# Linear attention with a SoLU feed-forward on one core: weights converted in 1024-column pieces, and a new written-out order

## The chip, the cores and the metric

The kernel runs on one core of a Trainium2 chip. The metric is the device time in microseconds (us); the lower the better. PE is the matrix engine (TensorE), DVE the vector engine, ACT the scalar engine (ScalarE), POOL is GpSimd, and SP issues the DMAs. Each engine works through its own instructions strictly in order.

## The reference

```python
# q, k, v: (8 batches, 8 heads, 576, 64) float32; the weights are float64
q_s = softmax(q, axis=-1)                    # exp(q - max), divided by the sum + 1e-9
k_s = softmax(k, axis=2)                     # over the 576 positions
kv  = einsum('bhsd,bhse->bhde', k_s, v)
x   = einsum('bhsd,bhde->bhse', q_s, kv)     # then to (8 * 576, 512)
h   = x @ w_in                               # (4608, 1024)
solu = h * softmax(h, axis=-1)
ln  = (solu - mean) / sqrt(var + 1e-6) * g_ln
out = ln @ w_out                             # (4608, 512)
```

## The kernel before

The work is cut into 36 row tiles of 128 rows: four for each of the 8 batches, and one for each pair of batches, made of the 64 rows that each has left over. There is one generator for each piece of work, and one step of a generator issues one or a few instructions. The string `ORDER` (1,509 items) says, by hand, which generator makes its next step; a suffix `.v` or `.p` moves that step's elementwise instruction to DVE or POOL. So the order on every engine, and often the engine, is written out in `ORDER`.

The names in it, and in the rows below:

- `LQ`, `LK`, `LV`, `V`, `LG`: loads of q, k, v and of the gain. `Q0a`, `Q1c`, `R1`: softmax of q (tiles `qm`, `qr`, maxima `qnmx`, sums `qsum`), split into a high and a low float16 half (`qhl`) and transposed by DMA into `qT`.
- `K0`: k's softmax of batch 0 (`km`, and `kr` for the 64 left-over rows; `khalf` and `ktop` are its maxima, `turned`, `col`, `wide`, `kb` carry them across partitions), the products `kv` with v, and its two float16 halves in a block diagonal (`bd`).
- `w0`, `w1`, ...: a piece of w_in. The host's float64 arrives as pairs of 32-bit words (tile `w_in`), and `float_of` puts a float32 together from them in `iw`: one instruction on ACT, a clamp on POOL or DVE, a shift and two merges on DVE. `W` scales w_in by a power of two and splits it into a high and a low float16 half (`wi`); it needs the largest value of the whole matrix (`m_in`), so all of w_in has to be converted first. `y0`, `y1`, ... and `Z` are the same for w_out (`w_out`, `gw`, `wo`).
- `x3`, `h3`, `o3`: for row tile 3 the product with `kv` (`xT`), the hidden layer with SoLU and the centred values (`h`, its maximum `top`, `nm`, `e`, `u`, transposed by DMA into `uT`), and the projection (`o`, `os`). Each of the products of `h` and `o` is three float16 products. `h` has two buffers in PSUM, `o` one.
- `P`: four products on zeros, to keep PE busy (`warm_up`).

For each tile of `h`, four single-column steps (`am`, `pi`, `p`, `ph`) run mostly on POOL, between DVE's `nm` and DVE's product `e`.

`BUFS` holds the number of buffers of `uT`, `xT` and of the words of a weight. The buffers of `uT` (4 KB in each partition) also hold w_in's words and the float32 weights.

## Time and profile before

| | |
|---|---|
| median of 3 runs | 533.48 us (533.06 to 534.55) |
| profiled execution, its own time | 535.23 us |
| its span, first to last instruction | 533.5 us |
| busy: PE, DVE, ACT, POOL | 475.2, 427.7, 270.4, 192.7 us |

Busy time is the time in which an engine executes an instruction; what matters is whether the engine that others wait for is busy at that place. In the page's picture of the span in 40 slices (busy tenths; PEclk is the clock that was granted to PE), the first quarter looks different from the rest:

```profile
PE   4652579889999999999999999999989999999886
DVE  4999999998899899899999999388978764635711
PEclk9576699998999999999999999999999999999999
```

### The profile page before, as it was taken

The numbers are of one execution on the slowest core, as the hardware profiler recorded it, in microseconds if no ns is written. First come the engines' busy times: TensorE is split into PE (matmuls) and PEld (weight loads), VectorE is DVE, ScalarE is ACT, GpSimd is POOL, SyncE is SP. The second block draws the span as 40 slices with busy tenths as digits, with TensorE's granted clock in tenths as the row PEclk, the third lists the DMA queues.
The fourth block names the chain that finished last, engine by engine and source line by source line (L and its number), as shares of the span: only waits on it lengthen the run. The fifth ranks groups of instructions, "written<-read, shape, count | busy, mean of one in ns | idle before, by whom it ended". The sixth has DMA issues, their size and how long they took to land.

```text
span 533.5 us, 8255 instructions
## 1 busy us (share of the span) xinstructions
PE 475.2 (89%) x3048; PEld 243.5 (46%) x3048; DVE 427.7 (80%) x724; ACT 270.4 (51%) x405; POOL 192.7 (36%) x309
## 2 busy tenths in 40 slices
PE   4652579889999999999999999999989999999886
PEld 1330245444454445455545455454445554544334
DVE  4999999998899899899999999388978764635711
ACT  2375556766474573456545656166645552424600
POOL 4522156543433550446334434054641321211210
PEclk9576699998999999999999999999999999999999
DMA  8963952992359957945965897179247443232251
GB/s 229 336 174 117 256 122 53 267 175 39 80 131 245 215 100 164 247 104 119 236 159 90 208 187 169 39 132 224 59 104 187 78 98 80 39 80 61 54 123 41
DMA packets 159240, 74.99 MB, mean 141 GB/s; under 512 B 127840, under 2 KB 152672, under 8 KB 159200
## 3 DMA queue, kind: packets, MB, share of 16 engines
q1 hardware_dynamic: 159200, 74.47, 62.1%
q8 instruction: 24, 0.39, 0.3%
q14 instruction: 16, 0.13, 0.1%
HBM read 36.70 MB, written 9.44 MB: 86 GB/s over the span
## 4 chain that ended last, share of the span: by engine, by line
PE 41%; DVE 38%; issue 8%; POOL 5%; ACT 4%; DMA 2%; SPq 0%; DVEq 0%; POOLq 0%; ACTq 0%
PE o L590 21%; PE h L519 17%; DVE e L548 4%; DVE top L526 4%; DVE km L356 3%; DMA qm<-in_q_dram 2%; DVE qsum L419 2%; DVE u L555 2%; POOL p L542 2%; DVE bd L395 2%; DVE qhl L430 1%; DVE qnmx L412 1%; DVE iw L237 1%; PE x L471 1%; DVE qden L421 1%
## 5 line engine op out<-in xcount | busy, mean ns | idle before, releaser
L519 PE MATMUL h<-wi,xT 128*128 128x512 f16 x864 | 196.4, 381 | 4.5 <-DVE e L548 4.0
L590 PE MATMUL o<-wo,uT 128*128 128x512 f16 (+1 forms) x888 | 194.2, 373 | 6.4 <-DVE os L598 4.2
L590 PEld LDWEIGHTS <-uT 128*128 128x128 f16 x888 | 85.9, 98 | 102.5 <-issue 7.6
L519 PEld LDWEIGHTS <-xT 128*128 128x128 f16 x864 | 83.7, 98 | 102.3 <-issue 3.2
L553 ACT ACTIVATE u<-e,nmu 128x1024 f16<-128x1024 f32 x36 | 41.3, 1148 | 33.8 <-DVE nmu L550 32.4
L526 DVE TENSOR_REDUCE top<-h 128x1 f32<-128x1024 f32 x36 | 43.8, 1216 | 17.3 <-PE h L519 17.2
L532 ACT ACTIVATE e<-h,nm,hs 128x1024 f32<-128x1024 f32 x32 | 38.5, 1203 | 33.3 <-DVE nm L528 32.0
L562 ACT ACTIVATE e<-e,nmu 128x1024 f32<-128x1024 f32 x36 | 41.2, 1146 | 25.7 <-DVE u L555 25.2
L555 DVE SCALAR_TENSOR_TENSOR u<-e,nmu,u 128x1024 f16<-128x1024 f32 x36 | 47.3, 1317 | 6.7 <-ACT u L553 6.7
L548 DVE SCALAR_TENSOR_TENSOR e<-h,ph,e 128x1024 f32<-128x1024 f32 x36 | 46.0, 1279 | 4.9 <-POOL ph L545 2.5
L575 POOL TENSOR_TENSOR r<-var,mhalf 128x1 f32<-128x1 f32 x36 | 24.4, 677 | 69.9 <-DVE var L572 63.6
L598 DVE TENSOR_SCALAR os<-o,rr 128x512 f32<-128x512 f32 (+1 forms) x21 | 15.2, 724 | 31.6 <-PE o L590 25.6
L503 ACT ACTIVATE xT<-x 128x512 f16<-128x512 f32 x36 | 21.2, 591 | 33.3 <-PE x L471 23.9
L542 POOL TENSOR_TENSOR p<-pi,mone 128x1 f32<-128x1 f32 x36 | 24.2, 673 | 34.1 <-DVE pi L539 32.5
L536 POOL TENSOR_SCALAR am<-nm 128x1 f32<-128x1 f32 x23 | 9.7, 422 | 67.7 <-DVE nm L528 67.6
L373 PE MATMUL kv<-vm,km 128*64 128x65 f32 x512 | 23.0, 234 | 7.5 <-ACT km L358 5.4
L471 PE MATMUL x<-qT,bd 128*128 128x128 f16 x128 | 23.8, 225 | 5.1 <-DVE bd L395 5.1
L416 ACT ACTIVATE qm<-qm 128x1024 f32<-128x1024 f32 (+1 forms) x17 | 17.1, 1007 | 19.4 <-DVE qm L414 12.7
L425 POOL TENSOR_TENSOR qm<-qm,qrec 128x1024 f32<-128x1024 f32 (+1 forms) x10 | 18.3, 1833 | 20.6 <-DVE qrec L423 12.9
L645 PE MATMUL warm_up<-bd 128*128 128x512 f16 x60 | 23.5, 535 | 2.3 <-POOL bd L127 1.7
L373 PEld LDWEIGHTS kv<-vm,km 128*64 128x64 f32 x512 | 18.5, 143 | 14.2 <-ACT km L358 5.9
L414 POOL TENSOR_TENSOR qm<-qm,qnmx 128x1024 f32<-128x1024 f32 (+1 forms) x8 | 15.3, 1907 | 25.9 <-DVE qnmx L412 21.4
(140 smaller groups left out, 698.8 us busy)
## 6 DMA issues: line engine op xcount, KB each, us to landing
...
w_in<-in_moe_w_in_dram SPq DMA_DIRECT2D x8, 512.0 KB, 9.2
w_out<-in_moe_w_out_dram SPq DMA_DIRECT2D x8, 512.0 KB, 5.5
out_dram<-os SPq DMA_DIRECT2D x10, 128.0 KB, 2.4
qm<-in_q_dram SPq DMA_DIRECT2D x2, 512.0 KB, 4.8
```

The source lines that it names most:

```text
L373: nc.tensor.matmul(o, km[:, h + i, c], vm[:, h + i, c], start=(c == 0), stop=False)
L471: nc.tensor.matmul(acc, al, bh, start=False, stop=True)
L519: nc.tensor.matmul(h[:, ns], xT[:, t, kc], wi[:, s, kc, ns], start=(kc == 0 and t == 0 and s == 0), stop=(kc == NP - 1 and t == 1),)
L526: nc.vector.tensor_reduce(top, h, axis=AX.X, op=ALU.max, negate=True)
L532: nc.scalar.activation(e, h, AF.Exp, bias=nm, scale=hs, accum_out=z)
L542: nc.gpsimd.tensor_tensor(p, pi, mone, op=ALU.pow)
L548: nc.vector.scalar_tensor_tensor(e, h, ph, e, op0=ALU.mult, op1=ALU.mult, accum_out=s1)
L553: nc.scalar.activation(u[:, 0], e, AF.Identity, bias=nmu)
L555: nc.vector.scalar_tensor_tensor(u[:, 1], e, nmu, u[:, 0], op0=ALU.add, op1=ALU.subtract)
L562: nc.scalar.activation(e, e, AF.Square, bias=nmu, accum_out=s2)
L575: nc.gpsimd.tensor_tensor(r, var, mhalf, op=ALU.pow)
L590: nc.tensor.matmul(o, uT[:, j, f], wo[:, s, f, cols], start=(f == 0 and j == 0 and s == 0), stop=(f == NF - 1 and j == 1))
```

## The change

Weights are loaded and converted in pieces of 1024 columns, so there are four pieces of w_in and four of w_out where there were eight of each. A piece is loaded by two DMAs of 512 KB, one step each, into one of two buffers of its own. In `float_of` the absolute value and the clamp go; ScalarE multiplies by 2^-112, which moves the exponent, and keeps the sign. The largest value of w_out is taken per piece and multiplied by the larger of the two gains. The products that spread k's maxima and the other single values over the partitions are issued as transposes. In `hidden`, the products with w_in's low half come last. The warm-up products write to the buffers of `h`. The order string is new (1,619 items).

```diff
-BUFS = 14, 4, 3
+BUFS = 12, 4, 2
 ORDER = (
-    "LG LQ0*2 w1 LK0*3 LV0 w0 w2 V00 V01 Q0b LV1 Q0b.v w4 Q0c Q0b w5 w7 Q0b Q0c w6 Q0a y0 y1 K0 Q0c y2 "
...
+    "LQ0*2 w0 Q0a Q0a.v LK0 w0 Q0b Q0a*2 Q0c w0 K0 w1 Q0a LK0 w0 Q0a K0 Q0b*2 w0*2 w1 V02 w2 Q0c Q0b "
...
     def largest(x, wide, name):
-        nc.tensor.matmul(wide, x.broadcast_to([P, P]), ident, start=True, stop=True)
+        nc.tensor.transpose(wide, x.broadcast_to([P, P]), ident)
...
-    def load_words(src, rows, cols, name, tag, bufs):
-        w = sb.tile([P, WN, 2], I32, name=f"w_{name}", tag=tag, bufs=bufs)
-        nc.sync.dma_start(out=w, in_=src[rows, 2 * cols.start : 2 * cols.stop].rearrange("p (n two) -> p n two", two=2))
-        return w
+    def load_words(src, n, name):
+        w = sb.tile([P, DF, 2], I32, name=f"w_{name}", tag="wd", bufs=WB)
+        for i, x in enumerate(src):
+            c = slice(i * n, (i + 1) * n)
+            nc.sync.dma_start(out=w[:, c], in_=x.rearrange("p (n two) -> p n two", two=2))
+            yield w
...
     def float_of(words, x):
-        nc.scalar.activation(x, high.bitcast(F32), AF.Abs)
-        yield
-        on(nc.gpsimd).tensor_scalar(x, x, 3.0e38, 1.125 * 2.0**-15, op0=ALU.min, op1=ALU.max)
-        yield
-        nc.vector.tensor_scalar(xi, xi, 3, 0x3FFFFFFF, op0=ALU.logical_shift_left, op1=ALU.bitwise_and)
+        nc.scalar.activation(x, high.bitcast(F32), AF.Copy, scale=2.0**-112)
+        yield
+        nc.vector.tensor_scalar(xi, xi, 3, 0x7FFFFFFF, op0=ALU.logical_shift_left, op1=ALU.bitwise_and)
         yield
         nc.vector.scalar_tensor_tensor(xi, low, 29, xi, op0=ALU.logical_shift_right, op1=ALU.bitwise_or)
         yield
-        nc.vector.scalar_tensor_tensor(xi, high, -0x40000000, xi, op0=ALU.bitwise_and, op1=ALU.bitwise_or)
+        nc.vector.scalar_tensor_tensor(xi, high, -0x80000000, xi, op0=ALU.bitwise_and, op1=ALU.bitwise_or)
...
-    def weight_in(i):
+    def weight_in(kc):
+        rows = slice(kc * P, (kc + 1) * P)
+        for words in load_words([w_in[rows, i * DF : (i + 1) * DF] for i in range(2)], DF // 2, f"in{kc}"):
+            yield
+        x = iw[kc] = sb.tile([P, DF], F32, name=f"iw{kc}", tag="uT", bufs=UB)
         yield from float_of(words, x)
-        junk = sb.tile([P, WN], F32, name=f"junk_in{i}", tag="os", bufs=2)
-        nc.scalar.activation(junk, x, AF.Abs, accum_out=iw["sum"][:, i : i + 1])
+        junk = sb.tile([P, DF], F32, name=f"junk_in{kc}", tag="e", bufs=3)
+        nc.scalar.activation(junk, x, AF.Abs, accum_out=iw["sum"][:, kc : kc + 1])
...
     def weights_in_scaled():
-        for i in range(NP * NB):
-            nc.scalar.activation(wi[:, 0, kc, ns], x, AF.Copy, scale=s)
+        for kc in range(NP):
+            nc.scalar.activation(wi[:, 0, kc], iw[kc], AF.Copy, scale=s)
             yield
-            nc.vector.scalar_tensor_tensor(wi[:, 1, kc, ns], x, s, wi[:, 0, kc, ns], op0=ALU.mult, op1=ALU.subtract)
+            nc.vector.scalar_tensor_tensor(wi[:, 1, kc], iw[kc], s, wi[:, 0, kc], op0=ALU.mult, op1=ALU.subtract)
...
     def weights_out_scaled():
+        nc.vector.tensor_reduce(
+            g2, gl.rearrange("p (i two) -> p i two", two=2), axis=AX.X, op=ALU.max, apply_absolute_value=True
+        )
+        nc.vector.tensor_tensor(g2, g2, gw["sum"], op=ALU.mult)
...
     def tops_of(top, b):
-            nc.tensor.matmul(wide[:, i], col[:, i : i + 1].broadcast_to([P, P]), ident, start=True, stop=True)
+            nc.tensor.transpose(wide[:, i], col[:, i : i + 1].broadcast_to([P, P]), ident)
...
     def hidden(row_tile):
-        for kc in range(NP):
-            for t, s in ((0, 0), (0, 1), (1, 0)):
+        terms = [(kc, t, s) for kc in range(NP) for t, s in ((0, 0), (1, 0))] + [(kc, 0, 1) for kc in range(NP)]
+        for i, (kc, t, s) in enumerate(terms):
...
     def warm_up():
-            acc = ps.tile([P, DM], F32, name=f"warm_up{len(warmed)}", tag="o", bufs=1)
+            acc = ps.tile([P, DF], F32, name=f"warm_up{len(warmed)}", tag="h", bufs=2)[:, 0:DM]
```

The new order at three places. First DVE, ahead of the largest value of w_in (`m_in`), where the last pieces of w_in are converted. Before:

```order
L235 TENSOR_SCALAR gw_311<-gw_311 128x512
L237 SCALAR_TENSOR_TENSOR gw_311<-w_out_143,gw_311 128x512
L239 SCALAR_TENSOR_TENSOR gw_311<-w_out_143,gw_311 128x512
L146 COPY vm<-v_3_221 128x8x64
L232 TENSOR_SCALAR iw_213<-iw_213 128x512
L235 TENSOR_SCALAR iw_213<-iw_213 128x512
L237 SCALAR_TENSOR_TENSOR iw_213<-w_in_154,iw_213 128x512
L239 SCALAR_TENSOR_TENSOR iw_213<-w_in_154,iw_213 128x512
L235 TENSOR_SCALAR gw_326<-gw_326 128x512
L237 SCALAR_TENSOR_TENSOR gw_326<-w_out_149,gw_326 128x512
L260 TENSOR_REDUCE m_in<-iw_sum 128x1
```

The same place on DVE now:

```order
L358 TENSOR_TENSOR km_105<-km_105,kb_220 128x1024
L363 TENSOR_TENSOR kr_154<-kr_154,kb_220 64x512
L242 SCALAR_TENSOR_TENSOR iw_204<-w_in_139,iw_204 128x1024
L244 SCALAR_TENSOR_TENSOR iw_204<-w_in_139,iw_204 128x1024
L240 TENSOR_SCALAR iw_233<-iw_233 128x1024
L242 SCALAR_TENSOR_TENSOR iw_233<-w_in_212,iw_233 128x1024
L244 SCALAR_TENSOR_TENSOR iw_233<-w_in_212,iw_233 128x1024
L414 TENSOR_REDUCE qnmx_2_315<-qm_238 128x16
L414 TENSOR_REDUCE qnmx_0_322<-qm_238 128x16
L261 TENSOR_REDUCE m_in<-iw_sum 128x1
```

The pieces of w_out that stood between those of w_in are gone from here (the first of them now follows the first `top`), a piece is twice as wide, and a clamp is no longer there.

Second SP, which issues the loads of w_in; `kr` is k's left-over rows. Before, behind the first loads of q, k and v:

```order
L221 DMA w_in_109<-in_moe_w_in_dram 128x1024
L221 DMA w_in_111<-in_moe_w_in_dram 128x1024
L184 DMA v_0_113<-in_v_dram 128x2x256
L184 DMA v_1_115<-in_v_dram 128x2x256
L197 DMA vr<-in_v_dram 64x8x64
L221 DMA w_in_121<-in_moe_w_in_dram 128x1024
L221 DMA w_in_126<-in_moe_w_in_dram 128x1024
L221 DMA w_in_128<-in_moe_w_in_dram 128x1024
```

SP now, from the second piece of w_in on (`w_in_139` is the third piece, `w_in_212` the fourth):

```order
L228 DMA w_in_124<-in_moe_w_in_dram 128x1024
L188 DMA v_2_137<-in_v_dram 128x2x256
L228 DMA w_in_139<-in_moe_w_in_dram 128x1024
L201 DMA kr_154<-in_k_dram 64x8x64
L228 DMA w_in_139<-in_moe_w_in_dram 128x1024
L454 DMA_TRANSPOSE qT_0_168<-qhl_0_129 128x8x128 x2
L188 DMA v_1_207<-in_v_dram 128x2x256
L228 DMA w_in_212<-in_moe_w_in_dram 128x1024
L188 DMA v_0_227<-in_v_dram 128x2x256
L228 DMA w_in_212<-in_moe_w_in_dram 128x1024
```

All of w_in was issued in one go; now q's transposes stand ahead of the last piece, and the third and fourth piece need a buffer of the first and second.

Third POOL, between the chain of the first hidden tile (`ph`) and that of the second (`am`). Before:

```order
L545 TENSOR_TENSOR ph_0_668<-p_0_659,hs_487 128x1
L414 TENSOR_TENSOR qr_401<-qr_401,qnmxr_661 128x512
L361 TENSOR_TENSOR kr_106<-kr_106,kb_681 64x512
L356 TENSOR_TENSOR km_460<-km_460,kb_681 128x1024
L536 TENSOR_SCALAR am_1_732<-nm_1_707 128x1
```

POOL now:

```order
L548 TENSOR_TENSOR ph_1_553<-p_1_548,hs_484 128x1
L358 TENSOR_TENSOR km_350<-km_350,kb_561 128x1024
L363 TENSOR_TENSOR kr_154<-kr_154,kb_561 64x512
L358 TENSOR_TENSOR km_350<-km_350,kb_561 128x1024
L432 TENSOR_TENSOR qhl_0_594<-qm_238,qhl_0_594 128x8x2x64
L539 TENSOR_SCALAR am_0_640<-nm_0_599 128x1
```

Both halves of batch 1's k subtraction are now POOL's, and a low part of q stands there too. Over the whole program, POOL has 9 such halves where it had 3 (DVE 7 where it had 13), and 24 full-width operations of q's maxima and sums where it had 16 (DVE 6 where it had 14). The warm-ups fall from 15 groups of four to 10. DVE's instructions fall from 690 to 640, counted with repeats.

More of the change, by code (lines that the diff above doesn't have):

```diff
@@ L274, in weights_in_scaled @@
             yield
-    gw = {"sum": cst.tile([P, NF], F32, name="gw_sum")}
+    gw = {"sum": cst.tile([P, NW], F32, name="gw_sum")}
     def load_gain():
         nc.sync.dma_start(out=gl, in_=g_ln.rearrange("(f p) -> p f", p=P))
-    def weight_out(f):
-        words = load_words(w_out, slice(f * P, (f + 1) * P), slice(0, DM), f"out{f}", "wd", WB)
-        yield
-        if f % 2 == 0:
-            gw[f] = sb.tile([P, 2, DM], F32, name=f"gw{f}", tag="uT", bufs=UB)
-            gw[f + 1] = gw[f]
-        col = slice(f, f + 1)
-        x = gw[f][:, f % 2]
-        yield from float_of(words, x)
-        junk = sb.tile([P, DM], F32, name=f"junk{f}", tag="os", bufs=2)
-        nc.scalar.activation(junk, x, AF.Abs, scale=gl[:, col], accum_out=gw["sum"][:, col])
@@ L294, in weights_out_scaled, with weight_out @@
-    def weights_out_scaled():
+    def weight_out(i):
+        blocks = [w_out[f * P : (f + 1) * P, :] for f in (2 * i, 2 * i + 1)]
+        for words in load_words(blocks, DM, f"out{i}"):
+            yield
+        x = gw[i] = sb.tile([P, 2, DM], F32, name=f"gw{i}", tag="uT", bufs=UB)
+        flat = x.rearrange("p f m -> p (f m)")
+        yield from float_of(words, flat)
+        junk = sb.tile([P, 2 * DM], F32, name=f"junk_out{i}", tag="e", bufs=3)
+        nc.scalar.activation(junk, flat, AF.Abs, accum_out=gw["sum"][:, i : i + 1])
@@ L462, in rest_queries @@
         yield from q_softmax(raw["qr"], parts, H, f"r{b}")
[L463 removed]
+        qT = qT_of["rest", b // 2] = sb.tile([P, 2, NP, P], F16, name=f"qTr{b}", tag="qTr", bufs=1)
         nc.sync.dma_start_transpose(
@@ L480, in scales @@
         if b % 2 == 1:
-            both = hs_of["rest"] = sm.tile([P, 1], F32, name=f"hsr{b}", tag="hsr", bufs=2)
+            both = hs_of["rest", b // 2] = sm.tile([P, 1], F32, name=f"hsr{b}", tag="hsr", bufs=2)
             nc.vector.tensor_copy(both[0:R], hs_of[b - 1][0:R])
@@ L493, in attend @@
         else:
-            groups = [(b - 1 + j, qT_of["rest"], slice(j * R, (j + 1) * R)) for j in range(2)]
+            groups = [(b - 1 + j, qT_of["rest", b // 2], slice(j * R, (j + 1) * R)) for j in range(2)]
         acc = ps.tile([P, NP, P], F32, name=f"x{name}", tag="att", bufs=3)
@@ L514, in hidden @@
         h = ps.tile([P, DF], F32, name=f"h{name}", tag="h", bufs=2)
-        for kc in range(NP):
-            for t, s in ((0, 0), (0, 1), (1, 0)):
-                for n in range(NB):
-                    ns = slice(n * 512, (n + 1) * 512)
-                    nc.tensor.matmul(
-                        h[:, ns], xT[:, t, kc], wi[:, s, kc, ns],
-                        start=(kc == 0 and t == 0 and s == 0), stop=(kc == NP - 1 and t == 1),
-                    )
-            yield
-        hs = hs_of["rest" if row_tile[1] == C else row_tile[0]]
+        terms = [(kc, t, s) for kc in range(NP) for t, s in ((0, 0), (1, 0))] + [(kc, 0, 1) for kc in range(NP)]
+        for i, (kc, t, s) in enumerate(terms):
+            for n in range(NB):
+                ns = slice(n * 512, (n + 1) * 512)
+                nc.tensor.matmul(
+                    h[:, ns], xT[:, t, kc], wi[:, s, kc, ns], start=(i == 0), stop=(i == len(terms) - 1)
+                )
+            if i % 2 == 1:
+                yield
+        hs = hs_of[("rest", row_tile[0] // 2) if row_tile[1] == C else row_tile[0]]
         top = sm.tile([P, 1], F32, name=f"top{name}", tag="htop")
@@ L670, in linear_attention_solu_ffn @@
             works[f"R{b}"] = rest_queries(b - 1)
-    for i in range(NP * NB):
+    for i in range(NP):
         works[f"w{i}"] = weight_in(i)
-    for f in range(NF):
-        works[f"y{f}"] = weight_out(f)
+    for i in range(NW):
+        works[f"y{i}"] = weight_out(i)
     works["Z"] = weights_out_scaled()
```

23 lines of the change are left out of this document (7 added, 16 removed), and 120 rows, old and new, of the table ORDER.

## The prediction

> **What bounds the kernel now.** I read the page's totals first, then a table by stretches of time, then the vector engine's (DVE) own rows up to the first hidden tile, and last the waits.
>
> ```profile
> span 533.5 us, 8255 instructions
> PE 475.2 (89%) x3048; PEld 243.5 (46%) x3048; DVE 427.7 (80%) x724; ACT 270.4 (51%) x405; POOL 192.7 (36%) x309
> ```
>
> PE and DVE are both near the span, so an average cannot say which of them counts. By stretches (columns: PE, PEld, DVE, ACT, POOL busy, then granted clock, DMA share, GB/s):
>
> ```profile
> 0.00:80.00 80.00, 43.77 (x234) 21.46 (x234) 70.48 (x113) 38.96 (x70) 29.82 (x29) 0.74 0.75 206
> 80.00:120.00 40.00, 34.64 (x282) 19.17 (x283) 37.30 (x66) 28.71 (x47) 21.94 (x37) 1.00 0.76 165
> 120.00:340.00 220.00, 215.19 (x1428) 111.11 (x1427) 198.91 (x335) 119.15 (x171) 86.78 (x131) 0.99 0.72 152
> 340.00:500.00 160.00, 156.28 (x971) 78.56 (x969) 111.52 (x195) 76.99 (x109) 50.56 (x102) 1.00 0.47 100
> 500.00:533.50 33.50, 25.30 (x138) 13.18 (x135) 9.50 (x18) 6.57 (x11) 3.57 (x12) 0.99 0.30 71
> ```
>
> Up to 80 us DVE is the bound. After that PE is idle only 5.4 + 4.8 + 3.7 + 8.2 = 22 us of 453.5. So the kernel is two runs in a row: DVE until the first hidden tile is finished, PE from there to the end. The seam is DVE's first maximum of a hidden tile (`top`):
>
> ```profile
> 7.16 0.69 DVE L412 TENSOR_REDUCE qnmx<-qm 128x8 f32<-128x512 f32 x1 [6.18 <-DMA qm<-in_q_dram]
> 7.88 0.69 DVE L414 TENSOR_TENSOR qm<-qm,qnmx 128x512 f32<-128x512 f32 x1
> 8.49 1.21 DVE L412 TENSOR_REDUCE qnmx<-qm 128x16 f32<-128x1024 f32 x1
> ...
> 79.99 1.23 DVE L526 TENSOR_REDUCE top<-h 128x1 f32<-128x1024 f32 x1
> ```
>
> DVE works almost without a pause from 7.16 to 79.99 us. Rows overlap slightly (the third starts before 7.88 + 0.69), so I take 0.93 of a sum of durations as elapsed time. Whatever DVE no longer does ahead of that row moves the seam, and all of PE's work behind it.
>
> **The change, part by part.** Rows that carry the prices (busy us, mean ns of one, then idle before):
>
> ```profile
> L356 DVE TENSOR_TENSOR km<-km,kb 128x1024 f32<-128x1024 f32 x13 | 20.4, 1569 | 2.5 <-ACT kb L332 2.5
> L548 DVE SCALAR_TENSOR_TENSOR e<-h,ph,e 128x1024 f32<-128x1024 f32 x36 | 46.0, 1279 | 4.9 <-POOL ph L545 2.5 <-ACT e L532 0.5 <-DVE ph L545 0.5
> L356 POOL TENSOR_TENSOR km<-km,kb 128x1024 f32<-128x1024 f32 x3 | 9.0, 2992 | 7.7 <-ACT kb L332 7.6
> L414 DVE TENSOR_TENSOR qm<-qm,qnmx 128x1024 f32<-128x1024 f32 x8 | 9.8, 1223 | 0.2
> L239 DVE SCALAR_TENSOR_TENSOR iw<-w_in,iw 128x512 int32<-128x512 int32 x8 | 8.4, 1046 | 0.3
> L273 DVE SCALAR_TENSOR_TENSOR wi<-iw,s_in,wi 128x512 f16<-128x512 f32 x8 | 6.0, 784 | 0.4 <-ACT wi L271 0.4
> L239 DVE SCALAR_TENSOR_TENSOR gw<-w_out,gw 128x512 int32<-128x512 int32 x8 | 5.9, 741 | 0.1
> L237 DVE SCALAR_TENSOR_TENSOR iw<-w_in,iw 128x512 int32<-128x512 int32 x8 | 5.8, 727 | 0.2
> L237 DVE SCALAR_TENSOR_TENSOR gw<-w_out,gw 128x512 int32<-128x512 int32 x8 | 5.5, 691 | 0.2
> L235 DVE TENSOR_SCALAR iw<-iw 128x512 int32<-128x512 int32 x8 | 5.2, 645 | 0.1
> L235 DVE TENSOR_SCALAR gw<-gw 128x512 int32<-128x512 int32 x8 | 4.2, 521 | 0.0
> L232 DVE TENSOR_SCALAR iw<-iw 128x512 f32<-128x512 f32 x5 | 3.5, 698 | 0.0
> L232 DVE TENSOR_SCALAR gw<-gw 128x512 f32<-128x512 f32 x2 | 0.8, 418 | 0.0
> ```
>
> *First term, DVE ahead of the seam.*
> - Five clamps of w_in disappear: −3.5 (the exponent is now moved by ScalarE's product, one instruction as before).
> - The w_out pieces that DVE converted ahead of the seam (one clamp, 4 shifts, 3 + 3 merges) now come behind it: 0.4 + 4 × 0.521 + 3 × 0.691 + 3 × 0.741 = −6.8. They are not saved, only put where PE already has work.
> - w_in's three conversions run 4 times on 1024 columns, not 8 times on 512. Before: 8 × (0.645 + 0.727 + 1.046) = 19.3. After: at most the same 19.3 for the same columns; at least 4 × 3 × 1.279 = 15.3 by the 1024-wide row L548. I take 16.5, near the row of the right width: −2.8.
> - w_in's low halves: 8 × 0.784 against 4 × 1.279: −1.2.
> - Batch 0: one half of k's subtraction goes to POOL, but the 64-row rest comes to DVE in return, which I count as nothing; other exchanges with POOL and ACT, one of batch 1's q subtractions (1.223) among them, come to about −2.
>
> Sum −16.3; times 0.93, −15.
>
> Against it stands a new wait. Words of a weight now lie in two buffers of 1024 columns, where there were 14 and 3 smaller ones. The third block of w_in is loaded only when DVE has finished the first, the fourth when it has finished the second, and SP issues in order: k's rest, v, and q's transposes are queued between and behind them.
>
> ```profile
> w_in<-in_moe_w_in_dram SPq DMA_DIRECT2D x8, 512.0 KB, 9.2
> kr<-in_k_dram SPq DMA_DIRECT2D x8, 128.0 KB, 7.0
> ```
>
> A load that is alone should land in less than that 9.2 us, which was measured with the queue full; following the order by hand, the fourth block is wanted about 8 us after its buffer is free. I charge 3 us, with 0 and 6 as bounds. **First term: −12; bounds −15.5 and −7.** The seam should be near 68 us.
>
> *Second term, PE behind the seam.* The replication of k's maxima becomes a transpose. Both forms stand side by side in the old trace:
>
> ```profile
> 131.85 5.34 PE L590 MATMUL o<-wo,uT 128*128 128x512 f16 x24
> 137.03 0.60 PE L322 MATMUL turned<-ident,ktop 128*128 128x128 f32 x4
> ...
> 143.29 1.05 PE L329 MATMUL wide<-ident,col 128*128 128x128 f32 x8
> ```
>
> ```profile
> L150 PE MATMUL kv<-ident,mx 128*128 128x128 f32 x16 | 4.1, 341 | 6.4 <-DVE mx L384 6.3
> L645 PE MATMUL warm_up<-bd 128*128 128x512 f16 x60 | 23.5, 535 | 2.3 <-POOL bd L127 1.7
> ```
>
> Four f32 products are 8 records and 1.05 us, four transposes 4 records and 0.60: −0.45 for each of 7 batches behind the seam = −3.2. The single replications (L150) drop from 2 records to 1: of 4.1 us at most half, so −1.3 behind the seam. PE is the bound there, so both count: **−4.5; bounds −2 and −5.3.** The order of `hidden`'s products (low weights last) changes no count: 24 of them per tile as before; it only lets a tile start before w_in's low halves are ready. Warm-ups fall from 60 to 40, 7.8 of the 23.5 us; they lie ahead of the first tile where PE waits for DVE, so I count nothing.
>
> *Third term, PE's idling behind the seam.* Over the whole program DVE loses 6 of 13 k subtractions (9.4 us), 8 of 14 full-width q operations (9.8 by L414), 7 clamps (4.3) and overheads of the conversions, nearly 30 us of 428. POOL takes the tensor work, at 2.992 for a k half. Between the first and the eighth `top` DVE has slightly less to do than before in spite of the w_out pieces that now stand there. Of the 5.4 + 4.8 + 3.7 us in which PE idled between 80 and 500 us **I take 2.5 off; bounds −8 and +2.** The last stretch is unchanged: the same four last projections, each behind the evacuation of the one before.
>
> Sum: 533.5 − 12 − 4.5 − 2.5 = 514.5 us of span. That execution took 535.2 us by its own time, 1.7 more than its span; the median of the runs shown is 533.48, which happens to be the span itself, so the forecast of the median is 514.5 too. A measurement of this kernel tells about 0.3% (1.6 us) from no change.
>
> **The page that speaks against it.** Operations of the two engines that meet hold each other up:
>
> ```profile
> 375.65 2.35 POOL L356 TENSOR_TENSOR km<-km,kb 128x1024 f32<-128x1024 f32 x1
> 376.56 2.52 DVE L356 TENSOR_TENSOR km<-km,kb 128x1024 f32<-128x1024 f32 x1
> ```
>
> DVE's subtraction takes about 1.2 us alone (the 1.223 of L414 is of the same width) and 2.52 when it starts under POOL's: it ends one undisturbed duration after POOL's end. By the Trainium skill, "SBUF — State Buffer", section "Who interferes with whom", the two engines share one port pair under an exclusive lock, taken by a DVE instruction with two SBUF inputs or in a two-port mode, and the loser blocks until the other's instruction ends. By that rule, the trace agrees.
>
> **The rivals.**
> 1. *POOL's extra work stalls DVE.* About 20 long tensor operations move to POOL; if each costs DVE the 1.3 us of the pair above, some at no meeting, say 0.5 to 0.8 us on average, that is 10 to 16 us. Ahead of the eighth `top` POOL has hardly more long operations than before (a k half more, the clamps gone), and later DVE runs ahead of PE, so I think most is covered. If half or more reaches the end: 514.5 + 5 to 16, about 524.
> 2. *Slower: a tile's chain stands behind POOL's k subtractions.* `am`, `pi`, `p`, `ph` of a tile run on POOL in order; DVE's product `e` waits for `ph`, it frees one of the two `h` buffers, PE waits for that. In the new order 10 us of POOL work (two k halves, k's rest, a q low part) stand between the first tile's `ph` and the second's `am`. DVE itself has about 10 us between the two tops, so a block of this size just fits; it decides when blocks come late by more than 19 us in sum. If each of the nine k halves on POOL holds one chain for its 2.992, 27 us are lost: 541. Against it:
>
> ```profile
> POOL am L536 <- DVE nm L528: 67.6, 17, 13.2
> DVE top L526 <- PE h L519: 17.2, 11, 3.6
> ```
>
> POOL idled 67.6 us waiting for DVE before these chains, so it was early as a rule.
>
> 3. *The clock.* With a third fewer warm-ups PE may reach the first tiles at the lower clock that the first stretch shows (0.74 granted on average). Early keys' products ran at 1.13 us for 16 and later ones at 0.69, so a tile's 5.3 us would be 8.7; two such tiles cost 7 us: 521. Against it: the last warm-ups still stand directly ahead of the first x products.
>
> ```profile
> 32.15 1.13 PE L373 MATMUL kv<-vm,km 128*64 128x65 f32 x16 [5.44 <-ACT km L358]
> 57.27 0.69 PE L373 MATMUL kv<-vm,km 128*64 128x65 f32 x16 [2.07 <-DVE vm L146]
> ```
>
> The Trainium skill, "TensorE: Matmul & The Clock Gate", section "Part 4: PE-mode transpose", says transposes do not count as activity for the clock in the way matmuls do, which would favour this rival; no trace here shows it.
>
> 4. *Nothing.* If the wait for w_in's blocks (two buffers) made the seam 15 us late, the first term would be 0; with the second at its bound of −2 and the third at +2 the time would be 533.5.
>
> **How the numbers follow.** The forecast as worked out, 0.64, by itself between 505 and 523; rival 1, 0.16; rival 2, 0.09; rival 3, 0.05; rival 4, 0.06. Faster by over 0.3%: 0.64 + 0.16 + 0.05 = 0.85; within: 0.06; slower: 0.09. The range for 8 in 10 joins the bounds, 533.5 − 15.5 − 5.3 − 8 = 505 and 533.5 − 7 − 2 + 2 = 526.5, and goes 2 us lower because DVE's conversions may be cheaper than the 1024-wide row: 503 to 527. Rivals 2 and 4 lie outside.
>
> **What will show it.** First term right: the first `top` on DVE starts near 68 us, with DVE's idle time behind a load of w_in under 6 us. Second: `wide` in 4 records of about 0.6 us. Third: PE idle behind the first `top` near 19 us. Rival 1 shows as a longer mean of DVE's k subtractions and two-input products; rival 2 as DVE's `e` waiting for POOL's `ph` far above 2.5 us; rival 3 as a granted clock under 1.0 behind the first tile. I am wrong if DVE, with less work, is later at the eighth `top` than before.

## The result, and the profile after

The median fell from 534.01 us (533.06 to 534.83, four runs) to 514.96 us (514.07 to 517.43, four runs) on the same chip: a ratio of 0.9651, with a 95% interval of 0.9613 to 0.9689. The forecast was 514.5. The profiled execution after took 514.96 us by its own time, with a span of 513.1 us; before, 535.23 and 533.5. The profiled execution of before lay 1.2 us above its median, so the two spans differ by 20.4 us where the medians differ by 19.05. One later run of the kernel before took 994 us and does not enter the ratios. The order strings have 1,450 and 1,556 items, not the 1,509 and 1,619 given further up.

The page of the kernel after, with its totals and three rows of the span in 40 slices:

```profile
PE 461.9 (90%) x2986; PEld 234.5 (46%) x2986; DVE 400.3 (78%) x674; ACT 261.8 (51%) x378; POOL 237.2 (46%) x316
...
PE   4075796899989999999999999999999999999986
DVE  4999999999989998989878896968876443455431
PEclk9578887999999999999999999999999999999999
```

DVE lost 27.4 us of busy time and POOL gained 44.5, but these totals do not say where the end moved. The slices say it better: PE's row of nines begins earlier. After the change the first `top` on DVE, the seam of the prediction, starts at 63.27 us. The table by stretches up to 120 us, cut there (columns: PE, PEld, DVE, ACT, POOL busy, then granted clock, DMA share, GB/s):

```profile
0.00:63.30 63.30, 31.97 (x206) 16.65 (x206) 54.05 (x78) 32.35 (x43) 29.74 (x23) 0.78 0.82 223
63.30:80.00 16.70, 14.50 (x104) 7.41 (x106) 16.44 (x16) 10.42 (x15) 14.16 (x9) 0.90 0.45 132
80.00:120.00 40.00, 35.65 (x237) 17.56 (x233) 38.73 (x70) 29.64 (x48) 19.23 (x36) 0.91 0.81 169
```

Three readings from it, against the same table of before:

- **Ahead of the seam** DVE's busy time fell from 70.48 to 54.05 us, by 16.4, and the seam came 16.7 us earlier (79.99 to 63.27). DVE's idle time there hardly changed: 80.0 − 70.5 = 9.5 us before, 63.3 − 54.05 = 9.25 after. A second profile of the same kernel (e9) has its seam at 65.32, so the shift is 14.7 to 16.7 us.
- **Behind the seam** the time went from 453.5 to 449.8 us, only 3.7 less. PE's busy time there went from 431.4 (475.18 − 43.77) to 429.9 (461.87 − 31.97), and its idle time from 22.1 to 19.9. In e9 the time behind is 448.1 us, with 429.8 busy and 18.3 idle.
- **The clock** granted to PE between the seam and 120 us was 1.00 before (80 to 120 us) and is 0.90 to 0.91 now. The cut at 120 us flatters the kernel before. Behind the seam PE runs at half clock for 3.41 + 6.83 = 10.24 us now, and before it did so for 3.41 us, from 119.95 on (the last microsecond of a span, in which PE has nothing to do, is left aside here and below):

```profile
63.80:67.21 3.41, 3.41 (x10) 1.33 (x9) 3.30 (x7) 1.29 (x2) 2.13 (x3) 0.50 0.68 142
80.87:87.70 6.83, 4.77 (x26) 1.84 (x21) 6.43 (x19) 3.96 (x6) 3.98 (x9) 0.50 1.14 195
```

```profile
119.95:123.36 3.41, 3.41 (x10) 1.21 (x8) 3.34 (x7) 3.33 (x6) 2.45 (x3) 0.50 0.41 80
```

So the forecast of the time was 0.5 us off, while two of its terms were each off by more: the first by 4.7 us (2.7 by e9), the second, in PE's busy time, by 3. They nearly cancelled, and that part of the agreement is luck.

DVE's own rows ahead of the seam (a bracket is the idle time before a row and what ended it):

```profile
6.12 0.69 DVE L414 TENSOR_REDUCE qnmx<-qm 128x8 f32<-128x512 f32 x1 [5.14 <-DMA qm<-in_q_dram]
...
10.84 1.24 DVE L347 TENSOR_TENSOR khalf<-km 128x512 f32<-128x512 f32 x1 [0.40 <-DMA km<-in_k_dram]
...
13.31 1.08 DVE L240 TENSOR_SCALAR iw<-iw 128x1024 int32<-128x1024 int32 x1 [1.23 <-ACT iw L238]
...
46.96 1.97 DVE L271 SCALAR_TENSOR_TENSOR wi<-iw,s_in,wi 128x1024 f16<-128x1024 f32 x1 [0.44 <-ACT wi L269]
...
63.27 1.23 DVE L529 TENSOR_REDUCE top<-h 128x1 f32<-128x1024 f32 x1
```

Apart from 0.79 us at the very start these are all the waits that the view lists up to the seam. The one at the start of w_in's conversions is 1.23 us, for the first block; the third and fourth block, for which the prediction charged 3 us, are not waited for here (in the repeated run e9 the fourth cost 0.51 us). DVE also starts 1.0 us earlier than before (6.12 against 7.16).

### The profile page after: what moved, and what is told of

It is laid out like the page before. It is cut to its first block, busy times and chain, and to the rows that moved or that the text cites. A ratio compares the mean times of both kernels' runs of the same rounds, so it can differ in the third digit from the quotient of the medians.

```text
span 513.1 us, 7978 instructions
## 1 busy us (share of the span) xinstructions
PE 461.9 (90%) x2986; PEld 234.5 (46%) x2986; DVE 400.3 (78%) x674; ACT 261.8 (51%) x378; POOL 237.2 (46%) x316
## 4 chain that ended last, share of the span: by engine, by line
PE 44%; DVE 38%; POOL 5%; DMA 4%; issue 4%; ACT 3%; SPq 1%; DVEq 0%; POOLq 0%; ACTq 0%
PE o L593 22%; PE h L522 18%; DVE e L551 3%; DVE top L529 3%; DVE u L558 3%; DVE qsum L421 3%; DVE vm L150 2%; DMA w_in<-in_moe_w_in_dram 2%; DVE khalf L347 2%; DVE wi L271 1%; DMA qm<-in_q_dram 1%; DVE qnmx L414 1%; PE kv L375 1%; DVE wo L312 1%; POOL km L358 1%
## 5 line engine op out<-in xcount | busy, mean ns | idle before, releaser
L522 PE MATMUL h<-wi,xT 128*128 128x512 f16 x864 | 204.9, 384 | 7.4 <-DVE e L551 4.9
L593 PE MATMUL o<-wo,uT 128*128 128x512 f16 (+1 forms) x888 | 199.2, 373 | 3.8 <-DVE os L601 3.2
L529 DVE TENSOR_REDUCE top<-h 128x1 f32<-128x1024 f32 x36 | 43.8, 1216 | 38.7 <-PE h L522 38.6
L558 DVE SCALAR_TENSOR_TENSOR u<-e,nmu,u 128x1024 f16<-128x1024 f32 x36 | 53.6, 1490 | 8.3 <-ACT u L556 8.2
L539 POOL TENSOR_SCALAR am<-nm 128x1 f32<-128x1 f32 x22 | 12.7, 577 | 77.7 <-DVE nm L531 66.0
L416 POOL TENSOR_TENSOR qm<-qm,qnmx 128x1024 f32<-128x1024 f32 (+1 forms) x13 | 26.6, 2050 | 29.0 <-DVE qnmx L414 29.0
L427 POOL TENSOR_TENSOR qm<-qm,qrec 128x1024 f32<-128x1024 f32 (+1 forms) x13 | 26.7, 2056 | 20.0 <-DVE qrec L425 15.5
L432 POOL TENSOR_TENSOR qhl<-qm,qhl 128x1024 f16<-128x1024 f32 (+1 forms) x12 | 25.9, 2162 | 16.8 <-ACT qhl L148 12.5
L603 ACT ACTIVATE os<-o,rr 128x512 f32<-128x512 f32 x23 | 15.7, 683 | 29.5 <-PE o L593 15.7
L375 PE MATMUL kv<-vm,km 128*64 128x65 f32 x512 | 22.1, 228 | 8.3 <-ACT vm L148 4.9
L418 ACT ACTIVATE qm<-qm 128x1024 f32<-128x1024 f32 (+1 forms) x17 | 16.9, 1000 | 22.1 <-POOL qm L416 15.9
L358 POOL TENSOR_TENSOR km<-km,kb 128x1024 f32<-128x1024 f32 x9 | 23.3, 2585 | 8.6 <-ACT kb L333 8.3
L507 DVE SCALAR_TENSOR_TENSOR xT<-x,xT 128x512 f16<-128x512 f32 x36 | 24.3, 681 | 3.4 <-ACT xT L505 3.3
```

The costliest lines, as they stand in the source:

```text
L358: on(nc.gpsimd).tensor_tensor(km[:, hs], km[:, hs], wide, op=ALU.subtract)
L375: nc.tensor.matmul(o, km[:, h + i, c], vm[:, h + i, c], start=(c == 0), stop=False)
L416: on(nc.gpsimd).tensor_tensor(x, x, wide(nmx), op=ALU.add)
L427: on(nc.gpsimd).tensor_tensor(x, x, wide(rec), op=ALU.mult)
L522: nc.tensor.matmul(h[:, ns], xT[:, t, kc], wi[:, s, kc, ns], start=(i == 0), stop=(i == len(terms) - 1))
L529: nc.vector.tensor_reduce(top, h, axis=AX.X, op=ALU.max, negate=True)
```

## The experiments

Each kernel was timed in five rounds beside the kernel before. "Seam" is the start of the first `top` in the profiled execution, "behind" is that execution's span less the seam. Lower ratios are better.

| kernel | ratio to before (95%) | median us | seam | behind |
|---|---|---|---|---|
| before | 1 | 534.0 to 534.4 | 79.99 | 453.5 |
| after | 0.9651 (0.9613 to 0.9689) | 514.96 | 63.3 | 449.8 |
| after, once more (e9) | 0.9657 (0.9626 to 0.9687) | 515.19 | 65.3 | 448.1 |
| e1: 4.9 us more for DVE ahead of the seam | 0.9727 (0.9708 to 0.9746) | 519.59 | 69.8 | 448.6 |
| e2: the same, late | 0.9672 (0.9656 to 0.9688) | 516.49 | 63.7 | 448.5 |
| e10: two pieces of w_out ahead of the seam again | 0.9723 (0.9703 to 0.9742) | 519.21 | 72.9 | 445.6 |
| e6: before, without clamps | 0.9883 (0.9863 to 0.9903) | 528.68 | 74.3 | 451.0 |
| e8: three word buffers | 0.9625 (0.9601 to 0.9648) | 514.63 | 63.2 | 447.7 |
| e11: conversions in halves | 0.9677 (0.9655 to 0.9699) | 517.69 | 64.9 | 452.1 |
| e5: before, with transposes | 0.9960 (0.9944 to 0.9975) | 532.27 | 79.3 | 451.1 |
| e4: after, without transposes | 0.9667 (0.9651 to 0.9684) | 515.99 | 64.2 | 450.8 |
| e3: PE kept busy at the seam | 0.9636 (0.9617 to 0.9655) | 514.46 | 63.8 | 447.7 |
| e7: all of k's subtractions on DVE | 0.9654 (0.9636 to 0.9672) | 516.28 | 63.3 | 450.0 |
| e12: e8 and e3 together | 0.9606 (0.9588 to 0.9625) | 513.13 | 63.2 | 447.6 |

In all of them the time behind the seam lies between 445.6 and 453.5 us, while the seam moves over almost 17 us. The kernel after, profiled twice, gave seams of 63.3 and 65.3: differences of the seam under 2 us say nothing.

### Is the seam the bound: the same work on DVE, early and late (e1, e2)

Four reductions whose result nobody reads are added to the kernel after, once ahead of the seam and once at the tiles 16 to 19.

```diff
+    def delay(times):
+        for _ in range(times):
+            d = sm.tile([P, 8], F32, name="delay", tag="delay", bufs=1)
+            nc.vector.tensor_reduce(d, ident.unsqueeze(1).broadcast_to([P, 8, P]), axis=AX.X, op=ALU.max)
...
         nc.vector.tensor_copy(isc, inv)
+        delay(4)          # e1; in e2 one each at the first step of h16, h17, h18, h19
```

> The changed kernel with four extra DVE reductions (1024 elements each, read from a constant, about 1.2 us each, 4.9 us together) right after w_in's scale is known, that is ahead of the first maximum of a hidden tile; nothing reads their result. Theory (two runs in a row, DVE up to the seam and PE behind it): the seam moves from 63.3 to about 68 us and the time from 515 to 519 to 520. Rival (DVE has slack even there, since PE idles through stalls of other kinds): the time moves by less than 2 us. If the low-half merges and the block diagonal that the extra work delays are not what PE waits for, it is also less than 2.

> The changed kernel with the same four extra DVE reductions, but one each at the start of row tiles 16 to 19 (about 245 to 290 us). Theory (PE is the bound behind the seam, DVE runs ahead of it): the time stays within 1 us of 515. Rival (DVE, 78% busy over the span, is still the bound here): up to 4.9 us more, 520.

Early, the 4.9 us cost 4.4 to 4.6 us of the median (3.7 to 4.1 by the ratios); late, 1.3 to 1.5 (0.8 to 1.1), with an interval that overlaps that of the kernel after. Ahead of the seam most of DVE's time is the kernel's time; at tiles 16 to 19 little or nothing of it is seen. In e1 the seam moved by 4.5 to 6.5 us and the time behind it stayed where it was.

### What moving w_out behind the seam was worth (e10)

The order of the kernel after is kept, but the conversions of two pieces of w_out go back ahead of the seam, among the steps that scale w_in (`W`), and their loads ahead of these.

```diff
+        early = {("w3", 5): ["y0"], ("w3", 6): ["y0", "y3", "y3"], ("W", 1): ["y0", "y3"],
+                 ("W", 4): ["y0"] * 3, ("W", 8): ["y3"] * 3}
+        skip, done = {"y0": 6, "y3": 6}, {}
         for item in order.split():
...
+                if skip.get(key, 0) > 0:
+                    skip[key] -= 1
+                    continue
                 step(key, engine)
+                done[key] = done.get(key, 0) + 1
+                for k in early.get((key, done[key]), []):
+                    step(k)
```

> The changed kernel with the conversion of the first two pieces of w_out (2 shifts and 4 merges of 1024 columns on DVE, 2 x (0.7 + 1.2 + 1.2) = 6.2 us) put back ahead of the seam, behind w_in's largest value, and their loads ahead of it; nothing is added or left out. Theory (work moved behind the seam is free, the prediction's largest single item, 6.8 us): the seam moves from 63.3 to about 69 us and the time by as much, 519 to 521. Rival (the work has to be done anyway and DVE is busy 95% of the time up to 120 us, so its place does not matter): less than 2 us.

The stretch up to its seam:

```profile
0.00:72.90 72.90, 34.62 (x206) 18.11 (x206) 60.68 (x84) 32.42 (x43) 28.84 (x23) 0.72 0.70 194
```

DVE has 6.6 us more to do there (60.68 against 54.05) and the seam is 7.6 to 9.6 us later, but only about 4 us of that reach the end: by the ratios (0.9723 − 0.9651 and − 0.9657) × 534 = 3.5 to 3.8, by the medians 4.0 to 4.3. Behind the seam this kernel needed 445.6 us, the least of all, 2.5 to 4.2 less than the two profiles of the kernel after. In part this can be w_out's work, which the kernel after does between its first tiles, where DVE's busy share is near one too (38.73 of 40 us between 80 and 120). But most of it is PE's busy time: 427.5 us behind the seam here, 429.9 and 429.8 in the kernel after. Here PE was at half clock for 3.41 us behind the seam, there for 10.24 in both profiles. PE's idle time is 18.1 us here, and 19.9 and 18.3 there. So the move of w_out was worth about 4 us, less than its 6.6 us of DVE's time; how much of the rest is work that comes back and how much is the clock is open.

### What the clamps were worth (e6)

The kernel before, with ScalarE's product in place of the absolute value and of the clamps, and nothing else.

```diff
-        nc.scalar.activation(x, high.bitcast(F32), AF.Abs)
+        nc.scalar.activation(x, high.bitcast(F32), AF.Copy, scale=2.0**-112)
...
-        on(nc.gpsimd).tensor_scalar(x, x, 3.0e38, 1.125 * 2.0**-15, op0=ALU.min, op1=ALU.max)
...
-        nc.vector.tensor_scalar(xi, xi, 3, 0x3FFFFFFF, ...)
+        nc.vector.tensor_scalar(xi, xi, 3, 0x7FFFFFFF, ...)
...
-        nc.vector.scalar_tensor_tensor(xi, high, -0x40000000, xi, ...)
+        nc.vector.scalar_tensor_tensor(xi, high, -0x80000000, xi, ...)
```

> The kernel before with ScalarE's product by 2^-112 in place of absolute value and clamp (16 clamps gone, 7 of them on DVE, 9 on POOL), pieces and order unchanged. The prediction's first item: DVE loses 3.5 us of w_in's clamps and 0.4 of w_out's ahead of the seam, times 0.93: the seam moves from 80 to about 76.5 us and the time from 533.7 to about 530. If POOL's clamps also were on the path of w_in's conversion (their steps stand between ACT's and DVE's), up to 2 us more. Rival (the order, not DVE's sum, sets the seam): less than 1 us.

```profile
0.00:74.30 74.30, 41.91 (x234) 21.41 (x234) 64.69 (x107) 38.75 (x70) 23.33 (x21) 0.77 0.82 221
```

The clamps alone were worth 5.7 us of the median (6.2 by the ratio), and 5.7 us of the seam. Their own durations on DVE were 3.9 us (3.5 for five of w_in, 0.4 for one of w_out). The other 1.9 of DVE's 5.8 us (70.48 − 64.69) came off instructions that stayed (the shift of w_in fell from 645 to 549 ns and its last merge from 1046 to 917, while the first merge rose from 727 to 781); POOL has 6.5 us less to do in the same stretch (29.82 to 23.33). Before, four of w_in's merges met a clamp on POOL and took 0.98 to 1.07 us, where an undisturbed one takes 0.69; no such row is left here. They account for about 1.3 of the 1.9 us.

### The wait for w_in's blocks (e8)

A third buffer for the words:

```diff
-BUFS = 12, 4, 2
+BUFS = 12, 4, 3
```

> The changed kernel with three buffers for a weight's words, so that the third block of w_in need not wait for the first to be converted. The prediction charged 3 us for that wait. If it was real: the seam up to 3 us earlier and the time about 512. By the changed kernel's trace DVE idled only about 1.6 us for loads ahead of the seam, all of it for the first block, which a third buffer does not help: the time stays within 1 us of 515. It may be longer if the earlier loads of w_in crowd out k and v.

SP's rows: w_in's third block and the row ahead of it in the kernel after, then the third block in this one:

```profile
5.85 0.68 SPq L188 DMA_DIRECT2D v<-in_v_dram  x1
18.15 0.33 SPq L228 DMA_DIRECT2D w_in<-in_moe_w_in_dram  x1
```

```profile
6.53 2.38 SPq L228 DMA_DIRECT2D w_in<-in_moe_w_in_dram  x1
```

With two buffers SP stood 11.6 us in front of the third block (6.5 to 18.15), and everything queued behind it stood too; with three it went on. The seam did not move (63.2). The wait that the prediction charged with 3 us existed, on SP, and cost nothing on DVE. In the profile of the kernel after, DVE's shift of the third piece starts at 28.38 us, 9 us behind the issue of the block's second half at 19.32, and such a load took 6.9 us to land (median). For the fourth piece the margin is small: issued at 28.78, wanted at 36.57, with ACT's instruction between.

### The width of a piece (e11)

The kernel after, with each of DVE's three conversions issued as two instructions of 512 columns.

```diff
-        nc.vector.scalar_tensor_tensor(xi, low, 29, xi, op0=ALU.logical_shift_right, op1=ALU.bitwise_or)
+        for c in halves:
+            nc.vector.scalar_tensor_tensor(
+                xi[:, c], low[:, c], 29, xi[:, c], op0=ALU.logical_shift_right, op1=ALU.bitwise_or
+            )
```

> The changed kernel with DVE's three conversions each issued as two instructions of 512 columns (pieces, loads and ScalarE's part stay 1024 wide). A merge measured 0.69 us at 512 columns and 1.21 at 1024 where nothing disturbed it, a shift 0.41 and 0.65: ahead of the seam 4 x (2 x 0.17 + 0.17) = 2 us more, 1.9 after overlap. Theory: seam and time 1.5 to 2 us later. Rival (the prediction's upper end, the same time for the same columns): no difference.

The two merges of w_in at 512 columns in this kernel, and below them the conversions of the kernel after:

```profile
L245 DVE SCALAR_TENSOR_TENSOR iw<-w_in,iw 128x512 int32<-128x512 int32 x8 | 5.1, 678 | 0.0
L250 DVE SCALAR_TENSOR_TENSOR iw<-w_in,iw 128x512 int32<-128x512 int32 x8 | 5.1, 678 | 0.0
```

```profile
L271 DVE SCALAR_TENSOR_TENSOR wi<-iw,s_in,wi 128x1024 f16<-128x1024 f32 x4 | 7.5, 1884 | 0.4 <-ACT wi L269 0.4
L244 DVE SCALAR_TENSOR_TENSOR iw<-w_in,iw 128x1024 int32<-128x1024 int32 x4 | 4.9, 1220 | 0.1
L242 DVE SCALAR_TENSOR_TENSOR iw<-w_in,iw 128x1024 int32<-128x1024 int32 x4 | 4.8, 1212 | 0.0
L240 DVE TENSOR_SCALAR iw<-iw 128x1024 int32<-128x1024 int32 x4 | 3.1, 766 | 1.2 <-ACT iw L238 1.2
```

Two merges of 512 take 1.36 us, one of 1024 takes 1.21 or 1.22: over w_in's eight merges at full width, 8 × 0.14 = 1.1 us. DVE is busy for 1.2 us more ahead of the seam (55.28 against 54.05), and the ratio is 1.1 to 1.4 us above that of the kernel after, with overlapping intervals. So the wide form explains little of the 6.5 us by which w_in's conversions became cheaper (19.3 to 4 × (0.766 + 1.212 + 1.220) = 12.8).

Most of the rest was visible before the change. DVE's conversions of w_in in the kernel before, and POOL's row at the same time:

```profile
24.18 2.50 DVE L239 SCALAR_TENSOR_TENSOR iw<-w_in,iw 128x512 int32<-128x512 int32 x1
...
28.12 0.69 DVE L237 SCALAR_TENSOR_TENSOR iw<-w_in,iw 128x512 int32<-128x512 int32 x1
...
29.45 0.42 DVE L235 TENSOR_SCALAR iw<-iw 128x512 int32<-128x512 int32 x1
```

```profile
23.57 2.55 POOL L430 TENSOR_TENSOR qhl<-qm,qhl 128x1024 f16<-128x1024 f32 x1
```

A merge of 512 columns takes 0.69 us by itself; under POOL's `qhl`, which ran to 26.12, it took 2.50. Undisturbed, a piece of 512 columns costs 0.42 + 0.69 + 0.69 = 1.80 us, eight of them 14.4; the old means add up to 19.3. The difference of 4.9 us is stall: seven of the 24 rows took over 0.25 us more than undisturbed, and each of the seven overlaps a row of POOL. The rows above show the longest. The remaining 1.6 (14.4 to 12.8) is the width. In the new order the means of the merges, 1212 and 1220 ns, are hardly above the shortest single one, 1.21.

### The transposes (e5, e4)

Added alone to the kernel before, and taken back alone in the kernel after:

```diff
-        nc.tensor.matmul(wide, x.broadcast_to([P, P]), ident, start=True, stop=True)
+        nc.tensor.transpose(wide, x.broadcast_to([P, P]), ident)
...
-            nc.tensor.matmul(wide[:, i], col[:, i : i + 1].broadcast_to([P, P]), ident, start=True, stop=True)
+            nc.tensor.transpose(wide[:, i], col[:, i : i + 1].broadcast_to([P, P]), ident)
```

> The kernel before with the replications of k's maxima and of the single values as transposes, nothing else changed. The second term alone: 533.5 - 4.5 = 529 if PE is the bound where they lie; by the changed kernel's trace, where only 1.5 us of PE busy time came off behind the seam, between 530 and 533.

> The changed kernel with the replications as f32 products again instead of transposes (undoes that part alone). The prediction's second term: 7 x 0.45 + 1.3 = 4.5 us more, 519.5, since PE is the bound behind the seam. Rival (PE's saving falls into gaps where it waits for DVE and k's chain anyway): less than 2 us more. The clock theory adds that products may hold the clock up better than transposes do, which would take up to 2 us off the loss.

The group of the replications in the kernel after, then without transposes (e4), and the second stretch of e4:

```profile
L330 PE MATMUL wide<-ident,col 128*128 128x128 f32 x32 | 5.3, 294 | 0.9 <-DVE col L326 0.9
```

```profile
L330 PE MATMUL wide<-ident,col 128*128 128x128 f32 x64 | 9.5, 297 | 0.9 <-DVE col L326 0.9
...
64.20:120.00 55.80, 49.58 (x333) 25.97 (x334) 54.25 (x83) 38.60 (x60) 33.44 (x44) 0.91 0.72 156
```

A replication is one record now where it was two, at the same duration for each. Added to the kernel before, the transposes gain 2.1 us (0.40%, interval 0.25 to 0.56%). In the kernel after, taking them back costs about 1 us of the median, which the interval cannot tell from nothing; PE's busy time behind the seam is 3.5 us longer without them (466.36 − 33.00 = 433.4 against 429.9). They take most of what the prediction said off PE's busy time (3.5 of 4.5 us), and half of it or less reaches the end, which is the rival's outcome.

### PE's clock behind the seam (e3)

24 more products on zeros, in three groups of eight: ahead of the first step of `h0`, of the 18th step of `K1` and of the first step of `h2`. Nobody reads their result.

```diff
+    extra = {("h0", 1): 2, ("K1", 18): 2, ("h2", 1): 2}
...
+            for _ in range(4):
+                nc.tensor.matmul(acc, bd[2][:, 0, 0], bd[2][:, 0].rearrange("p n k -> p (n k)"), start=True, stop=True)
```

> The changed kernel with 24 more products on zeros, in three groups of 8, at the three places where PE idles about 2 us each between 60 and 84 us and the granted clock falls (0.90 from 63 to 80 us, 0.91 from 80 to 120). Theory (the second term was mis-sized by the clock: some 60 matmuls of the first tiles ran at up to twice their later duration, 3 to 4 us): the time falls by 2 to 4 us, to 511 to 513, and the granted clock between 63 and 120 us rises above 0.97. Rival (PE waits for DVE there anyway, so a faster clock only makes the waits longer): within 1 us of 515, clock up all the same.

PE around the seam in the kernel after, and then in this one, with its second stretch:

```profile
62.24 0.61 PE L522 MATMUL h<-wi,xT 128*128 128x512 f16 x2 [2.12 <-DVE xT L507]
...
63.88 3.54 PE L522 MATMUL h<-wi,xT 128*128 128x512 f16 x8
67.26 0.60 PE L330 MATMUL wide<-ident,col 128*128 128x128 f32 x4
```

```profile
60.43 2.10 PE L662 MATMUL keep_warm<-bd 128*128 128x512 f16 x8
...
64.32 1.89 PE L522 MATMUL h<-wi,xT 128*128 128x512 f16 x8
...
63.80:120.00 56.20, 50.64 (x349) 25.21 (x350) 54.66 (x85) 40.01 (x62) 33.41 (x44) 1.00 0.72 160
```

The clock is back at 1.00, and the same eight products take 1.89 us where they took 3.54. The eight products alone would not show it, for in e9, the kernel after once more, they take 1.89 too, and its clock falls later, at 81.3 us, for 10.24. But e3 and e12 are the only profiles in which the clock does not fall anywhere behind the seam. PE's busy time behind the seam is 430.0 us, with 16 extra products in it; at 2.10 us for eight these are 4.2, so the rest is 425.8, 4.1 us less than in the kernel after (an estimate). The time itself moved by no more than 1 us in the median, inside the intervals, so the rival's outcome came and not the theory's 2 to 4 us. With the extra products counted as idle time, PE's idle time behind the seam is 447.7 − 425.8 = 21.9 us against 19.9 and 18.3: half or more of the time that the clock gave back went into longer waits.

### Does POOL's extra work hold DVE up at the end (e7)

All 16 halves of k's subtraction on DVE, none on POOL:

```diff
-            on(nc.gpsimd).tensor_tensor(km[:, hs], km[:, hs], wide, op=ALU.subtract)
+            nc.vector.tensor_tensor(km[:, hs], km[:, hs], wide, op=ALU.subtract)
```

> The changed kernel with all 16 halves of k's subtraction on DVE (9 of them go back from POOL). Theory: one half of batch 0 lies ahead of the seam and two of batch 1 shortly behind it, 1.25 us each, so 1 to 4 us more than 515; the other six lie where DVE runs ahead of PE. Rival 1 of the prediction (POOL's long operations stall DVE through the shared port): taking 23 us of them away makes up for DVE's own 11 us, and the time is the same or less.

Two of DVE's groups that have two inputs or a copy, in the kernel after, with that of `e` between them, and then in this one:

```profile
L558 DVE SCALAR_TENSOR_TENSOR u<-e,nmu,u 128x1024 f16<-128x1024 f32 x36 | 53.6, 1490 | 8.3 <-ACT u L556 8.2
L551 DVE SCALAR_TENSOR_TENSOR e<-h,ph,e 128x1024 f32<-128x1024 f32 x36 | 45.9, 1274 | 4.5 <-POOL ph L548 3.5 <-ACT e L535 0.2
L150 DVE COPY vm<-v 128x512 f32<-128x512 f32 x14 | 13.2, 948 | 0.0
```

```profile
L558 DVE SCALAR_TENSOR_TENSOR u<-e,nmu,u 128x1024 f16<-128x1024 f32 x36 | 51.6, 1436 | 8.3 <-ACT u L556 8.2
L150 DVE COPY vm<-v 128x512 f32<-128x512 f32 x14 | 10.8, 776 | 0.0
```

DVE has nine subtractions more, some 11 us at 1.22, and its busy time is no longer for it: 398.7 us, against 400.3 and 398.8 in the two profiles of the kernel after. What it takes over it regains in shorter stalls. The time stayed the same (0.9654 against 0.9651 and 0.9657). That is the outcome that the rival names; the theory's 1 to 4 us did not come clearly (1.1 to 1.3 by the medians). The stall on DVE is real. Whether it reaches the end this run cannot tell, since it takes stalls away and adds as much work in the same edit, and it takes back 22.3 of the 44.5 us that POOL gained.

### The best version (e12)

The third word buffer and the 24 products together.

> The changed kernel with three word buffers and the 24 products that keep PE warm, both of which came out 0.8 to 1.4 us faster, neither clear of the measurement. If both are real and lie in different places: 512.5 to 513.5, ratio to the kernel before near 0.960. If they were noise: 515.

513.13 us (512.59 to 513.58), a ratio of 0.9606. Beside the kernel after on the same chip (0.9657, from 0.9626) that is 0.5%, about 2.7 us; the one interval ends where the other begins. PE's products of `h`, 204.9 us in 864 records after, are 201.6 here, with the idle time ahead of them 3.5 instead of 7.4. Its interval still overlaps that of the first measurement of the kernel after, so the gain is at the edge of what can be told. Which of its two edits carries the gain is open: each alone stays inside the interval of the kernel after.

The repeated run of the kernel after, unchanged, set the scatter of the seam:

> The changed kernel itself, so that the three below are compared with it on the same chip: 515, seam near 63.3 us.

## Why the prediction was right, and where its terms were off

**Two runs in a row.** Shown. DVE's time counts ahead of the seam (e1) and hardly at tiles 16 to 19 behind it (e2), and the time behind stays within 8 us. The eighth `top`, which was to be the sign of a wrong prediction if it came later, starts at 132.1 us where it started at 156.0.

**First term, −12 forecast, −16.7 measured**, beyond its bound of −15.5 (−14.7 in e9, within it). Two steps failed.

- *The charge of 3 us for w_in's two buffers.* DVE waited 0.40 and 1.23 us near the first block and never for the later ones; the earlier start of q's load gave 1.0 back. The charge should have been about 0 (0.51 us in e9). I had followed when a block is issued late, 11.6 us on SP by e8, but had not set it against the time at which ACT and DVE come to it.
- *The prices of the conversions.* I took 16.5 us from "at most" the old means and "at least" the 1024-wide `e` row; 12.8 were measured, outside both bounds. The lower bound of 15.3 priced all three conversions at 1.279; the merges took 1.21 or 1.22, but the shift took 0.77, and that is 2.1 of the 2.5 us by which the bound was too high. The old means (727 and 1046 ns for two merges of the same shape) had waiting for POOL in them. Two equal shapes with different means were the sign, and the timeline had the undisturbed 0.69.

The term's largest item, the 6.8 us of w_out put behind the seam, brought about 4 at the end of the kernel (e10).

In the other direction, w_in's low halves were to fall from 6.3 to 5.1 us, and rose to 7.5; k's left-over rows, "counted as nothing", cost 2.85 for one instruction. Both are the same stall in the other place. `kr` and three of the four `wi` took about 5 us more than undisturbed rows of their shape (0.67 and 1.19 us; an estimate). DVE's rows after, and POOL's beside them:

```profile
31.41 2.85 DVE L363 TENSOR_TENSOR kr<-kr,kb 64x512 f32<-64x512 f32 x1
...
51.50 1.19 DVE L271 SCALAR_TENSOR_TENSOR wi<-iw,s_in,wi 128x1024 f16<-128x1024 f32 x1
...
53.21 2.32 DVE L271 SCALAR_TENSOR_TENSOR wi<-iw,s_in,wi 128x1024 f16<-128x1024 f32 x1
```

```profile
30.32 3.40 POOL L358 TENSOR_TENSOR km<-km,kb 128x1024 f32<-128x1024 f32 x1 [5.96 <-ACT kb L333]
...
51.73 2.72 POOL L427 TENSOR_TENSOR qm<-qm,qrec 128x1024 f32<-128x1024 f32 x1 [3.88 <-DVE qrec L425]
```

The `wi` that started 0.23 us ahead of POOL's `qm` took 1.19 us and made POOL's row longer (2.72, where another of its rows takes 1.90); the `wi` that started under it ended about one duration after POOL's end (51.73 + 2.72 = 54.45, and 53.21 + 2.32 = 55.53). `kr` did the same under POOL's `km`, which ran to 33.72. By the Trainium skill, "SBUF — State Buffer", section "Who interferes with whom", the order of issue decides which of the two engines blocks; the trace agrees, in both directions.

In durations, DVE's work up to the seam, the first `top` included, fell from 75.8 to 58.4 us: −3.9 for clamps, −6.6 for w_out, −6.5 for the conversions, +1.3 for the low halves, +1.6 for k (2.85 for `kr`, less one subtraction of 1.21), and −3.3 for other exchanges. That is −17.4 where the prediction had −16.3; the factor of 0.93 held (−16.2, and −16.4 measured as busy time).

**Second term, −4.5 forecast.** PE's work fell nearly as said: four records of 0.60 us for a batch, and 3.5 us of busy time in e4. But busy time behind the seam fell by only 1.5 in all, since PE was at half clock there for 10.24 us after and for 3.41 before. The difference of 6.83 us at half clock is worth about 3.4 us of products (an estimate). The term had no price for the clock; it stood only in rival 3, whose sign came true in a smaller size: 7 us were named, no more than 2 us of span separate the kernel after from e3, and 0.5 to 0.7 us of the median, inside the intervals. So by this estimate the clock accounts for what is missing of PE's busy time; what it cost the kernel is not shown. That the 20 warm-ups fewer are its cause, as rival 3 had it, was not shown: e5, with all 60, has 0.92 in the same stretch.

**Third term, PE's idling.** 22.1 to 19.9 us, −2.2 where −2.5 was forecast (18.3 in e9, −3.8). DVE runs further ahead of PE than before; waits of the kernel after:

```profile
POOL am L539 <- DVE nm L531: 66.0, 14, 11.7
...
DVE top L529 <- PE h L522: 38.6, 12, 6.5
```

DVE waited 17.2 us for PE's `h` before and waits 38.6 now.

**The rivals.** Rival 1, POOL's work stalling DVE: its mechanism is there (`u` 1317 to 1490 ns, `vm` 465 to 948). Ahead of the seam it is the 5 us of `kr` and `wi`, but the old order had as much in w_in's conversions. Behind the seam DVE runs ahead of PE, which speaks against an effect on the end; e7 found no gain from less work on POOL, but does not separate the two. Its listed sign, a longer mean of DVE's k subtractions, did not come (1569 to 1337), so that row was the wrong witness. Rival 2, the chain behind POOL's k subtractions: `e` waited 3.5 us for `ph` in all, and 2.5 before; POOL still waits 66 us for DVE's `nm` ahead of `am`. Rival 3: above. Rival 4, w_in's waits eating the first term: the seam at 63.3 and e8 exclude it.
